# Chunked attention and a multiplicative FFN: scores and values on 64x64 array tiles behind on-chip partition moves, FFN tiles of 512 tokens, first two pairs by halves of heads

## The chip, the cores and the metric

The kernel runs on one core of a Trainium2 chip. Its time is the device time of one execution in microseconds (us); the time before is the median of three executions. Profiles come from one further execution each, recorded by the hardware profiler, which has its own time.

A core has TensorE (PE) for matmuls, with the weight load as a second track (PEld), VectorE (DVE), ScalarE (ACT), GpSimd (POOL), which here only issues loads, and SyncE (SP), which issues the other transfers. Each engine takes its instructions in the order of the program. Matmuls write PSUM; ACT and DVE read it.

## The reference

Two parts follow each other. Attention is local: each of 8 batches x 8 heads has 576 positions of 64 features, cut into 9 chunks of 64 positions, and a position sees only its own chunk.

```python
q_c = q.reshape(B, H, nc, 64, D)          # k_c, v_c alike; B = H = 8, nc = 9, D = 64
scores = (1 / sqrt(D)) * q_c @ k_c.T      # 64 x 64 per chunk and head
attn = exp(scores - max); attn /= sum(attn) + 1e-9
x = (attn @ v_c) put as [4608 tokens, 512 features]
h = ((x @ w1) * (x @ w2)) @ w3            # w1, w2: 512 x 1024; w3: 1024 x 1024
out = h @ w_out                           # w_out: 1024 x 512, float32
```

Inputs and output are float32; inside, operands are bfloat16 and sums float32. Since nothing stands between w3 and w_out, the kernel multiplies these two first and applies their product.

## The kernel before

The 4608 tokens are 72 chunks of 64; two chunks make a unit, and two units make a *pair* of 256 tokens, so there are 18 pairs, 0 to 17. The work is cut into steps with one-letter names, and the string `ORDER` lists them all. A loop at the end of the kernel emits each step's instructions in that order, and a helper (`inorder`) holds the scheduler to it. So the order in `ORDER` is the order in every engine's queue. A step is written as letter, pair, and a second index, as in `T5.1`.

Loads, issued by POOL with a cast to bfloat16: `q`, `k`, `v` load one tensor of a pair, `l` all three; `i` loads a quarter of w1 and of w2, `o` loads w_out, `h` a half of w3. For pair 0 alone q and k come as raw float32 by SP and are cast by ACT (L131, L133).

Attention of a pair:

- `T` (L163): DVE transposes q (`T.0`) or k (`T.1`) in blocks of 32 x 32. The 64 features of a head thereby end as two blocks `e` of 32 over one set of 32 partitions; partition block i (of four) holds chunk i of the pair.
- `S` (L172): scores on PE, by head two steps e of contraction 32, for each of the four chunks: 64 matmuls of 32 rows x 64 columns of weights, 64 wide.
- `E` (L182): exp on ACT. `P` (L188): PE multiplies with v, which has a column of ones for the sums; the queries are cut in two blocks of 32, so 64 matmuls of 64 rows x 32 columns, 65 wide.
- `N` (L204): DVE takes the reciprocal of the sums and scales. `X` (L211): DVE transposes into `xt`, the FFN's right operand, which holds all tokens.

The FFN of a pair, in four steps j of two 128-row blocks of the hidden layer each:

- `A` and `B` (L227): x @ w1 and x @ w2, 8 matmuls each, 256 tokens wide. `C` (L242): ACT copies A's result out of PSUM. `M` (L246): DVE multiplies it with B's into `ab`.
- `O` (L263): PE multiplies `ab` with w3 @ w_out, 16 matmuls 512 wide. `Y` (L279): ACT copies it out and SP stores it. The last pair's O has three pieces with a copy and a store each, all in one PSUM tile.

`V`, `W`, `Z` make w3 @ w_out: DVE transposes w3, PE multiplies, ACT casts. `D` are matmuls on zeros, whose results are overwritten.

Everything on PE writes to one pool of four PSUM tiles (two banks each), taken in turn. Further rings: six qk buffers, seven v buffers, two `qkT`, two `o_sb`, seven `ab`.

In the steady part a pair p reads in `ORDER`: `P(p) M S(p+1) N(p).0 O(p-3) E(p+1) X(p).0 ... A B C M ...`; O of a pair stands right behind the pair's last M and the next S.

Of the kernel before, what the change touches and what calls it, by code (L numbers as in the profile page):

```python
# [9 lines left out]
l0 q1 i0 k1 v1 i1 i2 l2 i3 l3 l4 o h0 h1 l5 D0.0.16.64 T0.0 T0.1 l6 S0 T1.0 E0 P0 D0.1.4.512 T1.1 l7  # L10
N0.0 S1 D1.0.5.512 X0.0 N0.1 X0.1 A0.0 E1 B0.0 C0.0 P1 M0.0 A0.1 N1.0 X1.0 B0.1 C0.1 N1.1 A0.2 X1.1
B0.2 C0.2 M0.1 A1.0 T2.0 B1.0 C1.0 M0.2 A1.1 T2.1 l8 B1.1 C1.1 M1.0 S2 M1.1 A0.3 E2 T3.0 B0.3 C0.3
P2 M0.3 A1.2 N2.0 X2.0 B1.2 C1.2 N2.1 A1.3 X2.1 B1.3 C1.3 M1.2 A2.0 T3.1 l9 B2.0 C2.0 M1.3 S3 T4.0
A2.1 E3 M2.0 B2.1 T4.1 C2.1 P3 l10 M2.1 A2.2 N3.0 B2.2 C2.2 X3.0 A2.3 N3.1 B2.3 X3.1 C2.3 M2.2 S4
M2.3 A3.0 E4 B3.0 C3.0 A3.1 M3.0 B3.1 C3.1 V0 A3.2 M3.1 B3.2 C3.2 V1 A3.3 M3.2 B3.3 C3.3 V2 W0 M3.3
V3 T5.0 W1 Z0 V4 V5 T5.1 W2 Z1 V6 V7 T6.0 P4 l11 Z2 S5 T6.1 W3 E5 N4.0 X4.0 N4.1 X4.1 T7.0 A4.0 Z3
B4.0 T7.1 C4.0 P5 l12 M4.0 S6 N5.0 O0 E6 X5.0 N5.1 X5.1 T8.0 O1 Y0 T8.1 P6 l13 Y1 S7 N6.0 O2 E7 X6.0
N6.1 X6.1 T9.0 T9.1 O3 Y2 A4.1 Y3 B4.1 C4.1 A4.2 M4.1 B4.2 C4.2 A4.3 M4.2 B4.3 C4.3 P7 l14 M4.3 S8
N7.0 O4 E8 X7.0 N7.1 X7.1 T10.0 A5.0 T10.1 Y4 B5.0 C5.0 A5.1 M5.0 B5.1 C5.1 A5.2 M5.1 B5.2 C5.2 A5.3
M5.2 B5.3 C5.3 A6.0 M5.3 B6.0 C6.0 P8 l15 M6.0 S9 N8.0 O5 E9 X8.0 N8.1 X8.1 T11.0 A6.1 T11.1 Y5 B6.1  # L20
C6.1 A6.2 M6.1 B6.2 C6.2 A6.3 M6.2 B6.3 C6.3 P9 l16 M6.3 S10 N9.0 O6 E10 X9.0 N9.1 X9.1 T12.0 A7.0
T12.1 Y6 B7.0 C7.0 A7.1 M7.0 B7.1 C7.1 A7.2 M7.1 B7.2 C7.2 A7.3 M7.2 B7.3 C7.3 P10 l17 M7.3 S11
N10.0 O7 E11 X10.0 N10.1 X10.1 T13.0 A8.0 T13.1 Y7 B8.0 C8.0 A8.1 M8.0 B8.1 C8.1 A8.2 M8.1 B8.2 C8.2
A8.3 M8.2 B8.3 C8.3 P11 M8.3 S12 N11.0 O8 E12 X11.0 N11.1 X11.1 T14.0 A9.0 T14.1 Y8 B9.0 C9.0 A9.1
M9.0 B9.1 C9.1 A9.2 M9.1 B9.2 C9.2 A9.3 M9.2 B9.3 C9.3 P12 M9.3 S13 N12.0 O9 E13 X12.0 N12.1 X12.1
T15.0 A10.0 T15.1 Y9 B10.0 C10.0 A10.1 M10.0 B10.1 C10.1 A10.2 M10.1 B10.2 C10.2 A10.3 M10.2 B10.3
C10.3 P13 M10.3 S14 N13.0 O10 E14 X13.0 N13.1 X13.1 T16.0 A11.0 T16.1 Y10 B11.0 C11.0 A11.1 M11.0
B11.1 C11.1 A11.2 M11.1 B11.2 C11.2 A11.3 M11.2 B11.3 C11.3 P14 M11.3 S15 N14.0 O11 E15 X14.0 N14.1
X14.1 T17.0 A12.0 T17.1 Y11 B12.0 C12.0 A12.1 M12.0 B12.1 C12.1 A12.2 M12.1 B12.2 C12.2 A12.3 M12.2
B12.3 C12.3 P15 M12.3 S16 N15.0 O12 E16 X15.0 N15.1 X15.1 A13.0 Y12 B13.0 C13.0 A13.1 M13.0 B13.1  # L30
C13.1 A13.2 M13.1 B13.2 C13.2 A13.3 M13.2 B13.3 C13.3 P16 M13.3 S17 N16.0 O13 E17 X16.0 N16.1 X16.1
A14.0 Y13 B14.0 C14.0 A14.1 M14.0 B14.1 C14.1 A14.2 M14.1 B14.2 C14.2 A14.3 M14.2 B14.3 C14.3 P17
M14.3 A15.0 N17.0 X17.0 B15.0 C15.0 N17.1 O14 X17.1 M15.0 A15.1 Y14 B15.1 C15.1 A15.2 M15.1 B15.2
C15.2 A15.3 M15.2 B15.3 C15.3 A16.0 M15.3 B16.0 C16.0 O15 M16.0 A16.1 Y15 B16.1 C16.1 A16.2 M16.1
B16.2 C16.2 A16.3 M16.2 B16.3 C16.3 A17.0 M16.3 B17.0 C17.0 O16 M17.0 A17.1 Y16 B17.1 C17.1 A17.2
M17.1 B17.2 C17.2 A17.3 M17.2 B17.3 C17.3 M17.3 O17 Y17
# [4 lines left out]
def kernel(  # L41
# [11 lines left out]
    nc = tc.nc  # L53
# [12 lines left out]
    PT = 2 * UT  # L66
    NP = NT // PT
# [35 lines left out]
    xt = wpool.tile([P, KO, NT], bf, name="xt")  # L103
# [3 lines left out]
    vbuf = [consts.tile([P, 2, H, VW], bf, name=f"vbuf{i}") for i in range(7)]  # L107
# [16 lines left out]
    def load_qk(p, which=(0, 1)):  # L124
        if p not in qk_t:
            qk_t[p] = io.tile([P, 2, H, 2 * D], bf, tag="qk", bufs=6, name="qk")
        for s in which:
            if p == 0:

                raw = io.tile([P, H, 2 * D], f32, tag="raw", name="raw")  # L130
                inorder(nc.sync.dma_start(  # L131
                    raw[:], (q, k)[s][0, :, 0:4 * CH, :].rearrange("h (p t) d -> p h (t d)", t=2)))
                inorder(nc.scalar.copy(qk_t[p][:, s], raw[:]))  # L133
                continue
            for at, b, c, m in spans(4 * p, 4):
                load(qk_t[p][at * BL:(at + m) * BL, s],
                     (q, k)[s][b, :, c * CH:(c + m) * CH, :].rearrange("h (p t) d -> p h (t d)", t=2))

    def load_v(p):
        for u in range(2):  # L140
            for at, b, c, m in spans(4 * p + 2 * u, 2):
                load(vbuf[p % 7][at * CH:(at + m) * CH, u, :, 0:D],
                     v[b, :, c * CH:(c + m) * CH, :].rearrange("h p d -> p h d"))
# [17 lines left out]
    qkT_t, s_t, e_t, pv_t, xn_t = {}, {}, {}, {}, {}  # L161

    def do_T(p, s):  # L163


        if s == 0:
            qkT_t[p] = asb.tile([P, 2, 2, H, CH], bf, tag="qkT", bufs=2, name="qkT")
        inorder(nc.vector.transpose(  # L168
            qkT_t[p][:, s].rearrange("p e h (y t) -> p h t e y", t=2),
            qk_t[p][:, s].rearrange("p h (t e y) -> p h t e y", t=2, e=2)))  # L170

    def do_S(p):  # L172
        qkT = qkT_t.pop(p)
        s_t[p] = s_t.pop(p) if p in s_t else psum("s_ps")
        for h in range(H):
            for e in range(2):
                for i in range(NB):
                    mm(s_t[p][half[i % 2], i // 2, h * CH:(h + 1) * CH],
                       lhsT=qkT[blk[i], 1, e, h, :],
                       rhs=qkT[blk[i], 0, e, h, :], start=(e == 0), stop=(e == 1))  # L180

    def do_E(p):  # L182
        e_t[p] = asb.tile([P, 2, H, CH], bf, tag="e", bufs=2, name="e")
        inorder(nc.scalar.activation(  # L184
            e_t[p][:].rearrange("p u h q -> p u (h q)"), s_t.pop(p)[:],
            Exp, scale=scale, bias=0.0))

    def do_P(p, u):  # L188
        e = e_t[p] if u == 0 else e_t.pop(p)
        pv = pv_t[p, u] = psum("pv")  # L190
        for n in range(2):
            for qh in range(2):
                for g in range(NB):
                    for r in range(2):
                        at = (2 * qh + n) * W
                        mm(pv[blk[g], r, at:at + W],
                           lhsT=e[half[r], u, 2 * g + n, qh * BL:(qh + 1) * BL],
                           rhs=vbuf[p % 7][half[r], u, 2 * g + n, 0:W], start=True, stop=True)

    def do_P2(p):  # L200
        do_P(p, 0)
        do_P(p, 1)

    def do_N(p, u):  # L204
# [3 lines left out]
        xn_t[p, u] = asb.tile([P, 2, 4, D], bf, tag="xn", bufs=2, name="xn")  # L208
        inorder(nc.vector.tensor_mul(xn_t[p, u][:], pv[:, :, :, 0:D], rc.to_broadcast([P, 2, 4, D])))  # L209

    def do_X(p, u):  # L211
        t0 = p * PT + u * UT
        inorder(nc.vector.transpose(  # L213
            xt[:, :, t0:t0 + UT].rearrange("p o (m y) -> p m o y", y=BL),
            xn_t.pop((p, u))[:].rearrange("p r (c n) (z o) -> p (r c) o n z", c=2, o=KO)))

    ab_t, ps_t, a_t = {}, {}, {}
# [9 lines left out]
    def mm_ab(p, j, which):  # L227
        w = (w1, w2)[which]
        for i in range(2):
            for ki in range(KO):  # L230
                mm(ps_t[p, j][:, which, i * PT:(i + 1) * PT],
                   lhsT=w[:, ki, (2 * j + i) * P:(2 * j + i + 1) * P],
                   rhs=xt[:, ki, p * PT:(p + 1) * PT], start=(ki == 0), stop=(ki == KO - 1))

    def do_A(p, j):
        ps_t[p, j] = ps_t.pop((p, j)) if (p, j) in ps_t else psum("ab_ps")
        mm_ab(p, j, 0)

    def do_B(p, j):
        mm_ab(p, j, 1)  # L240
# [5 lines left out]
    def do_M(p, j):  # L246
        if p not in ab_t:
            ab_t[p] = msb.tile([P, FO, PT], bf, tag="ab", bufs=7, name="ab")
        inorder(nc.vector.tensor_mul(  # L249
            ab_t[p][:, 2 * j:2 * j + 2, :].rearrange("p j t -> p (j t)"), a_t.pop((p, j))[:],  # L250
            ps_t.pop((p, j))[:, 1, :]))

    def store(p, u0, u1, n0, n1, o_sb):
        inorder(nc.sync.dma_start(
            out[p * PT + u0 * UT:p * PT + u1 * UT, n0:n1].rearrange("(u p) n -> p u n", p=UT),
            o_sb[:, u0:u1, n0:n1]))

    def mm_o(p, u, n0, n1):
        for ki in range(FO):
            mm(ps_t[p][:, u, n0:n1], lhsT=ab_t[p][:, ki, u * UT:(u + 1) * UT],  # L260
               rhs=w3o[:, ki, n0:n1], start=(ki == 0), stop=(ki == FO - 1))

    def do_O(p):  # L263
        ps_t[p] = psum("o_ps")
        if p < NP - 1:
            for u in range(2):
                mm_o(p, u, 0, DM)
# [89 lines left out]
```

The softmax here doesn't subtract the row's maximum and nothing guards it: scores larger than these inputs give would overflow.

## Time and profile before

| what | value |
|---|---|
| time before, median of 3 | 254.39 us (254.19 to 254.47) |
| the profiled execution, its own time | 254.46 us |
| its span, first to last instruction | 252.7 us |
| granted PE clock | 0.998 of full speed |
| PE busy | 234.9 us, 3841 matmuls |
| DVE, ACT, POOL busy | 156.4, 86.3, 82.9 us |
| DMA of POOL's queue | 18.88 MB written, 82592 packets |
| DMA of SP's queue | 10.49 MB |
| HBM read and written | 38.80 MB, 9.44 MB |

The busiest groups of instructions, as count, busy time and mean duration of one:

| instructions | count | busy us | mean ns |
|---|---|---|---|
| matmuls of A and B, 256 wide | 1136 | 128.0 | 273 |
| matmuls of O, 512 wide | 280 | 63.2 | 379 |
| matmuls of S | 1024 | 11.3 | 193 |
| matmuls of P | 1152 | 12.7 | 197 |
| DVE transposes T | 36 | 45.1 | 1287 |
| DVE products M | 71 | 48.3 | 682 |
| DVE transposes X | 36 | 25.6 | 712 |
| DVE products of N | 36 | 24.9 | 692 |
| ACT copies C | 71 | 41.6 | 586 |
| stores of a pair, 512 KB, issue to landing | 17 | | 4000 |

How to read this. The span lies inside the execution's own time; the rest is before its first and after its last instruction. A matmul's mean duration is longer than its share of PE's time, because matmuls overlap: what counts is the distance between the starts of two. Busy shares are averages over stages. The chain of waits starts at the last instruction and goes back, at each step, to what released it; a piece of the chain carries its start and duration. A window of the timeline merges equal instructions into one line, with start, duration and count. "Idle" of an engine that nobody waits for costs nothing.

### The profile page before, as it was taken

To read this page: it belongs to the slowest core of one execution; us is meant where nothing else is said; L and a number is where in the kernel's file an instruction comes from. 1 tells how busy PE (TensorE), PEld (TensorE's weight loads), DVE (VectorE), ACT (ScalarE), POOL (GpSimd) and SP (SyncE) were. 2 spreads that over 40 slices of the span, in tenths; PEclk is the share of its full clock that TensorE was granted. 3 is DMA by queue.
4 is the path that set the end of the run, shared out by engine and by line. 5 is a ranking of instruction groups with operands and counts; after the bars stand their busy time and mean duration, and the time that the engine had idled before them with its cause. 6 is when DMAs were issued, how large, how long until landed. Compare 5 with 4: busy or idle time off the path is not lost.

```text
span 252.7 us, 8382 instructions
## 1 busy us (share of the span) xinstructions
PE 234.9 (93%) x3841; PEld 170.5 (67%) x3841; DVE 156.4 (62%) x233; ACT 86.3 (34%) x116; POOL 82.9 (33%) x110
## 2 busy tenths in 40 slices
PE   1389999999899999999999999999999999999993
PEld 1237878854555577866868686868686868678662
DVE  1665999699996457486665758584945445432230
ACT  3312424432433343333334243343334332323321
POOL 8756975657984567654020000000000000000000
PEclk9999999999999999999999999999999999999999
DMA  7999999999999999999953020202021120102022
GB/s 177 182 184 177 182 175 202 196 184 167 175 170 214 244 227 182 199 167 148 187 38 92 3 83 4 86 3 86 5 81 44 46 81 5 64 22 84 0 86 83
DMA packets 89763, 29.90 MB, mean 118 GB/s; under 512 B 73728, under 2 KB 85248, under 8 KB 89728
## 3 DMA queue, kind: packets, MB, share of 16 engines
q0 software_dynamic: 82592, 18.88, 80.4%
q1 hardware_dynamic: 7136, 10.49, 11.8%
q8 instruction: 30, 0.49, 0.7%
q14 instruction: 5, 0.04, 0.0%
HBM read 38.80 MB, written 9.44 MB: 191 GB/s over the span
## 4 chain that ended last, share of the span: by engine, by line
PE 65%; DMA 14%; DVE 10%; POOL 4%; ACT 3%; issue 3%; DVEq 0%; POOLq 0%
PE ab_ps L88 39%; PE o_ps L88 25%; DMA w<-in_moe_w_dram 4%; DVE ab L249 4%; DMA qk<-in_q_dram 4%; DMA qk<-in_k_dram 3%; DVE w3T L290 3%; DMA vbuf<-in_v_dram 3%; ACT a_sb L244 3%; POOL w L91 1%; DVE qkT L168 1%; POOL vbuf L91 1%; POOL qk L91 1%; POOL wo L91 1%; DVE xt L213 1%
## 5 line engine op out<-in xcount | busy, mean ns | idle before, releaser
L88 PE MATMUL ab_ps<-xt,w 128*128 128x256 bf16 x1136 | 128.0, 273 | 1.3 <-DVE xt L213 1.3
L88 PEld LDWEIGHTS <-w 128*128 128x128 bf16 x1152 | 112.3, 98 | 19.4 <-DVE xt L213 2.4
L249 DVE TENSOR_TENSOR ab<-a_sb,ab_ps 128x512 bf16<-128x512 f32 x71 | 48.3, 682 | 71.6 <-ACT a_sb L244 71.6
L244 ACT COPY a_sb<-ab_ps 128x512 f32<-128x512 f32 x71 | 41.6, 586 | 79.3 <-PE ab_ps L88 79.3
L88 PE MATMUL o_ps<-w3o,ab 128*128 128x512 bf16 (+1 forms) x296 | 65.3, 373 | 2.7 <-ACT o_sb L276 1.1
L88 PEld LDWEIGHTS <-ab 128*128 128x128 bf16 x296 | 28.7, 97 | 33.3 <-issue 1.6
L168 DVE STREAM_TRANSPOSE qkT<-qk 128x1024 bf16<-128x1024 bf16 x36 | 45.1, 1287 | 8.5 <-ACT qk L133 5.1
L91 POOL DMA_DIRECT2D vbuf<-in_v_dram x40 | 33.9, 852 | 31.3 <-PE pv L88 16.3
L283 ACT COPY o_sb<-o_ps 128x1024 f32<-128x1024 f32 x17 | 17.2, 1014 | 45.9 <-PE o_ps L88 43.2
L213 DVE STREAM_TRANSPOSE xt<-xn 128x512 bf16<-128x512 bf16 x36 | 25.6, 712 | 1.2
L209 DVE TENSOR_TENSOR xn<-pv,rc 128x512 bf16<-128x512 f32 x36 | 24.9, 692 | 1.2
L91 POOL DMA_DIRECT2D qk<-in_q_dram x23 | 18.1, 793 | 6.8 <-DMA qk<-in_k_dram 2.4
L184 ACT ACTIVATE e<-s_ps 128x1024 bf16<-128x1024 f32 x16 | 16.4, 1025 | 8.7 <-PE s_ps L88 8.4
L91 POOL DMA_DIRECT2D qk<-in_k_dram x23 | 18.0, 788 | 3.3 <-DMA w<-in_moe_w_dram 1.7
L88 PEld LDWEIGHTS <-qkT 32*64 32x64 bf16 x1152 | 11.4, 111 | 10.6 <-DVE qkT L168 9.6
L88 PE MATMUL w_ps<-wo,w3T 128*128 128x512 bf16 x64 | 14.2, 379 | 0.0
L88 PEld LDWEIGHTS <-e 64*32 64x32 bf16 x1152 | 10.1, 90 | 5.5 <-issue 3.6
L88 PE MATMUL pv<-vbuf,e 64*32 64x65 bf16 x1152 | 12.7, 197 | 1.1 <-ACT e L184 1.1
L91 POOL DMA_DIRECT2D w<-in_moe_w_dram x16 | 11.1, 697 | 5.4 <-DMA wo<-in_moe_w_out_dram 3.0
L88 PE MATMUL s_ps<-qkT 32*64 32x64 bf16 x1024 | 11.3, 193 | 0.0
L88 PEld LDWEIGHTS <-w3T 128*128 128x128 bf16 x64 | 6.2, 98 | 7.1
L290 DVE STREAM_TRANSPOSE w3T<-w 128x1024 bf16<-128x1024 bf16 x8 | 9.6, 1211 | 0.9 <-DMA w<-in_moe_w_dram 0.9
(20 smaller groups left out, 33.9 us busy)
## 6 DMA issues: line engine op xcount, KB each, us to landing
out_dram<-o_sb SPq DMA_DIRECT2D x17, 512.0 KB, 4.0
vbuf<-in_v_dram POOLq DMA_DIRECT2D x32, 128.0 KB, 6.7
w<-in_moe_w_dram POOLq DMA_DIRECT2D x16, 256.0 KB, 9.9
qk<-in_q_dram POOLq DMA_DIRECT2D x11, 256.0 KB, 6.6
qk<-in_k_dram POOLq DMA_DIRECT2D x11, 256.0 KB, 8.0
wo<-in_moe_w_out_dram POOLq DMA_DIRECT2D x4, 256.0 KB, 6.9
qk<-in_q_dram POOLq DMA_DIRECT2D x4, 192.0 KB, 9.4
qk<-in_k_dram POOLq DMA_DIRECT2D x4, 192.0 KB, 8.7
```

Source lines behind the costliest of these rows:

```text
L88: return inorder(nc.tensor.matmul(*a, **kw))
L91: return inorder(nc.gpsimd.dma_start(dst, src))
L168: inorder(nc.vector.transpose(qkT_t[p][:, s].rearrange("p e h (y t) -> p h t e y", t=2), qk_t[p][:, s].rearrange("p h (t e y) -> p h t e y ...
L184: inorder(nc.scalar.activation(e_t[p][:].rearrange("p u h q -> p u (h q)"), s_t.pop(p)[:], Exp, scale=scale, bias=0.0))
L209: inorder(nc.vector.tensor_mul(xn_t[p, u][:], pv[:, :, :, 0:D], rc.to_broadcast([P, 2, 4, D])))
L213: inorder(nc.vector.transpose(xt[:, :, t0:t0 + UT].rearrange("p o (m y) -> p m o y", y=BL), xn_t.pop((p, u))[:].rearrange("p r (c n) (z o) ...
L244: inorder(nc.scalar.copy(a_t[p, j][:], ps_t[p, j][:, 0, :]))
L249: inorder(nc.vector.tensor_mul(ab_t[p][:, 2 * j:2 * j + 2, :].rearrange("p j t -> p (j t)"), a_t.pop((p, j))[:], ps_t.pop((p, j))[:, 1, :]))
L283: inorder(nc.scalar.copy(o_sb[:], ps_t.pop(p)[:]))
L290: inorder(nc.vector.transpose(w3T_t[f][:].rearrange("p k (f y) -> p f k y", y=BL), w3[:, NB * f:NB * (f + 1), :].rearrange("p f (k x) -> p ...
```

## The change

Four things change together, with a new `ORDER`.

1. *First two pairs by halves of heads.* `q`, `k`, `T`, `S`, `E`, `P` of pairs 0 and 1 come twice, with four heads each. q and k of pair 0 are loaded by POOL like all others; the raw transfers on SP and the casts on ACT are gone. Of the zero matmuls `D`, 32 of 64 columns stay ahead of S0; those of 512 columns ahead of A0.0 are gone.
2. *From pair 8 on, q, k and x of two pairs change partitions.* A group g is two pairs, 2g and 2g+1; `qkT` now holds both pairs of a group. `G` (new) moves it by SP transfers from `qkT` to `qkm`, so that the two blocks e of a head's features stand one above the other on 64 partitions. A score then needs one matmul of 64 x 64 instead of two of 32 x 64. `P` takes all 64 queries of a chunk as weights: 64 x 64. Its output then has another layout, so `X` writes to `xm`, and `H` (new) moves that to `xt` by SP transfers. Each `G` and each `H` has two halves of four transfers: 32 partitions of 4 KB each (128 KB) for G, of 2 KB each (64 KB) for H.
3. *Loads run five pairs ahead*, with five qk and six v buffers instead of six and seven.
4. *FFN tiles of 512 tokens from pair 4 on.* A and B work for a whole group, 8 steps j with one 128-row block each: 4 matmuls of 512 columns. `ab` and `xt` become rings by group (three and four buffers). From pair 8 on M writes `ab` in runs of 32 tokens to undo the order that H left. O stands later, apart from its M. The store of `Y` becomes a step of its own, `Q`. The last O's three pieces take a PSUM tile each, and Y16 with its Q16 stands behind that O.

The diff, cut to its core:

```diff
 ORDER = """
-l0 q1 i0 k1 v1 i1 i2 l2 i3 l3 l4 o h0 h1 l5 D0.0.16.64 T0.0 T0.1 l6 S0 T1.0 E0 P0 D0.1.4.512 T1.1 l7
...
-C10.3 P13 M10.3 S14 N13.0 O10 E14 X13.0 N13.1 X13.1 T16.0 A11.0 T16.1 Y10 B11.0 C11.0 A11.1 M11.0
...
-M17.1 B17.2 C17.2 A17.3 M17.2 B17.3 C17.3 M17.3 O17 Y17
+q0.0 k0.0 q0.1 k0.1 v0 q1.0 q1.1 k1.0 k1.1 i0 v1 q2 k2 i1 v2 i2 i3 q3 k3 v3 o h0 h1 q4 k4 v4
+D0.0.32.64 T0.0.0 T0.1.0 T0.0.1 S0.0 T0.1.1 q5 k5 v5 E0.0 S0.1 E0.1 P0.0 P0.1 T1.0.0 N0.0 T1.1.0
+T1.0.1 S1.0 T1.1.1 q6 k6 v6 E1.0 X0.0 S1.1 N0.1 X0.1 P1.0 E1.1 T2.0 A0.0 T2.1 q7 k7 B0.0 C0.0 P1.1
+v7 M0.0 A0.1 N1.0 B0.1 C0.1 X1.0 S2 N1.1 E2 M0.1 X1.1 P2 A1.0 N2.0 B1.0 X2.0 C1.0 A1.1 N2.1 B1.1
...
+M3.2 B3.3 C3.3 V3 W0 M3.3 T4.0 W1 Z0 V4 V5 T4.1 q9 k9 v9 W2 Z1 V6 V7 T5.0 S4 Z2 W3 T5.1 q10 k10 E4
+T6.0 T6.1 P4 v10 q11 k11 Z3 S5 N4.0 O0 E5 X4.0 N4.1 X4.1 T7.0 O1 T7.1 Y0 Q0 T8.0 P5 v11 q12 k12 Y1
+S6 T8.1 O2 Q1 E6 N5.0 X5.0 N5.1 X5.1 O3 T9.0 T9.1 Y2 G4.0 P6 v12 q13 k13 A4.0 N6.0 B4.0 G4.1 Y3 X6.0
+N6.1 C4.0 A4.1 X6.1 B4.1 C4.1 M4.0 Q2 S7 Q3 M4.1 A4.2 E7 T10.0 B4.2 C4.2 T10.1 P7 v13 q14 k14 A4.3
+M4.2 B4.3 N7.0 C4.3 A4.4 X7.0 M4.3 B4.4 C4.4 N7.1 A4.5 M4.4 B4.5 C4.5 X7.1 S8 M4.5 S9 E8 A4.6 T11.0
...
+M16.6 B16.7 C16.7 O13 M16.7 O14 Y13 Q13 O15 Y14 Q14
+O16 Y15 Q15 O17 Y16 Q16 Y17 Q17
 """
...
+    def move(dst, src):
+        inorder(nc.sync.dma_start(dst, src))
...
+    def do_G(g, a):
+        if a == 0:
+            qkm_t[g] = asb.tile([P, 2, 2, 2, H, CH], bf, tag="qkm", bufs=2, name="qkm")
+        for i in (2 * a, 2 * a + 1):
+            for e in range(2):
+                move(qkm_t[g][blk[2 * a + e], i % 2], qkT_t[g][blk[i], e])
...
+            else:                                                     # do_S, pair 8 on
+                for i in (0, 3, 1, 2):
                     mm(s_t[p][half[i % 2], i // 2, h * CH:(h + 1) * CH],
+                       lhsT=qkm_t[g][half[i // 2], i % 2, m, 1, h, :],
+                       rhs=qkm_t[g][half[i // 2], i % 2, m, 0, h, :], start=True, stop=True)
...
+                else:                                                 # do_P, pair 8 on
+                    for g, r in ((0, 0), (1, 1), (1, 0), (0, 1)):
+                        mm(pv[half[g], r, m * W:(m + 1) * W], lhsT=e[half[r], u, 4 * g + m, :],
+                           rhs=vbuf[p % 6][half[r], u, 4 * g + m, 0:W], start=True, stop=True)
...
+    def do_H(g, a):
+        xt = new_xt(g)[:].rearrange("p (s c) -> p s c", s=2)
+        for k_ in range(2):
+            for i in (2 * a, 2 * a + 1):
+                move(xt[blk[2 * a + k_], i % 2], xm_t[g][blk[i], k_].rearrange("p o m t -> p (o m t)"))
...
+    def do_AB(p, j, f, which):
...
+        fs = (f,) if p >= 4 else (2 * j, 2 * j + 1)
+        n = GT // len(fs)
+        for i, f in enumerate(fs):
             for ki in range(KO):
+                mm(ps_t[p, j][:, which, i * n:(i + 1) * n],
+                   lhsT=(w1, w2)[which][:, ki, f * P:(f + 1) * P], rhs=rhs[:, ki],
+                   start=(ki == 0), stop=(ki == KO - 1))
...
+        else:                                                         # do_M, pair 8 on
+            o = ab_t[g][:, j].rearrange("p (c s y) -> p s c y", s=2, y=BL)
+            view = lambda t: t.rearrange("p (s c y) -> p s c y", s=2, y=BL)
+        inorder(nc.vector.tensor_mul(o, view(a_t.pop((p, j))[:]), view(ps_t.pop((p, j))[:, 1, :])))
...
+            t = psum("o_ps")                                          # do_O, last pair: a tile for each piece
+            mm_o(t[:, 0, 0:n1 - n0], p, u, n0, n1)
+            inorder(copy(o_sb[:, u, n0:n1], t[:, 0, 0:n1 - n0]))
+            store(p, u, u + 1, n0, n1, o_sb[:, u:u + 1, n0:n1])
```

## The prediction, made before the changed kernel ran

> **What bounds the kernel now.** I read the engine shares first, then the busy times by stage, then the chain of waits, then the rows of single steps on TensorE (PE), last the DMA rows. The two page lines show PE busy for 93% of the span, and the DMA engines nearly full for the first half of it.
>
> ```profile
> PE 234.9 (93%) x3841; PEld 170.5 (67%) x3841; DVE 156.4 (62%) x233; ACT 86.3 (34%) x116; POOL 82.9 (33%) x110
> DMA  7999999999999999999953020202021120102022
> ```
>
> The stages (busy time of each engine in a stretch) say where PE is not full: 10.5 us before 18.26, under 1 us in each stretch up to 212, and 4.5 us at the end. From 18.26 to 212 the path is PE's own instructions, one after the other.
>
> ```profile
> 0.00:18.26 18.26, 7.78 (x217) 4.51 (x218) 8.96 (x18) 5.43 (x5) 12.75 (x21) 1.00 1.44 181
> 18.26:52.25 33.99, 33.33 (x641) 28.15 (x640) 27.21 (x40) 11.87 (x18) 23.83 (x33) 1.00 1.66 187
> 52.25:68.29 16.04, 15.38 (x194) 7.26 (x191) 15.90 (x20) 5.28 (x6) 12.18 (x16) 1.00 1.99 173
> 68.29:128.10 59.81, 59.28 (x1008) 41.54 (x1008) 39.71 (x57) 21.40 (x28) 32.41 (x41) 1.00 1.66 187
> 128.10:212.00 83.90, 82.98 (x1457) 62.77 (x1456) 52.30 (x80) 30.69 (x42) 1.76 (x2) 1.00 0.18 49
> 212.00:252.70 40.70, 36.17 (x330) 26.21 (x328) 12.27 (x20) 11.62 (x18) 0.00 (x0) 0.99 0.14 53
> ```
>
> The chain gives the price of each PE step: P and S 0.63 and 0.64 us (64 small matmuls each), A and B together 7.00 us for 64 of 256 columns (109 ns each), O 3.45 us for 16 of 512 columns (216 ns each). It also shows, once in every pair, a detour over ACT and DVE ahead of O: O waits for the last product M.
>
> ```profile
> 78.68 0.63 PE pv L88 x64
> 79.30 0.64 PE s_ps L88 x64
> ...
> 121.19 7.00 PE ab_ps L88 x64
> 128.20 0.02 issue
> 128.22 0.59 ACT a_sb L244
> 128.81 0.02 issue
> 128.84 0.70 DVE ab L249
> 129.53 0.04 issue
> 129.58 3.61 PE o_ps L88 x16
> ...
> 225.07 3.45 PE o_ps L88 x16
> ```
>
> **Small matmuls (pairs 8 to 17).** S falls from 64 matmuls of 32 rows by 64 to 32 of 64 by 64; P from 64 of 64 by 32 to 32 of 64 by 64. Whether half the count takes half the time depends on what paces a block. Two timeline answers, cut off at 128.90 and 128.19, count the matmuls started from the block's start to the cut:
>
> ```profile
> 128.74 0.35 PE L88 MATMUL s_ps<-qkT 32*64 32x64 bf16 x20
> 128.11 0.26 PE L88 MATMUL pv<-vbuf,e 64*32 64x65 bf16 x17
> ```
>
> S starts 20 in 160 ns on four tiles: one round of four each 32 ns. P starts 17 in 80 ns on eight tiles: a round of eight each 35 to 40 ns. So a round costs some 32 to 40 ns however many tiles it has, and the count alone does not pace it. The new blocks have 8 rounds of four tiles: 8 x 32 = 0.26 us, and the 0.13 us that S has beyond its 16 rounds (0.64 - 16 x 0.032): 0.385 us for S, 0.39 for P. Saved: 10 x (1.27 - 0.775) = 5.0 us, all on the path. Bounds: half of the old time, 6.3 us; nothing, 0. A rule speaks against it: by the Trainium skill, "TensorE: Matmul & The Clock Gate", section "The mechanism", a weight load overlaps running matmuls only in other row groups, and by "LDWEIGHTS (loading the stationary operand)" 64 columns take 64/1.2 = 53 ns. Two of the four new tiles share each half of the rows, so a round would be an estimated 2 x (53 + 64/2.4 = 27 of streaming) = 160 ns and a block 1.28 us: 20 blocks x 0.64 = 12.8 us lost, and the sum below would end at 266. The P row says no: four tiles share a row half there, 128 weight columns per half and round as in the new form, in 35 to 40 ns. I take the row.
>
> **512-column tiles.** 14 pairs from pair 4 on trade 64 matmuls of 109.1 ns for 32 of 215.7: 6.98 - 6.90 = 0.08 us each, 1.1 us. ACT copies and DVE products stay 512 wide, at 586 and 682 ns against a PE step of 1.73 us for A and B. From pair 8 M writes runs of 32 elements; the nearest row is the strided xn product of the same size, 692 ns, so I cost it at nothing, hidden by PE; at 900 ns DVE would come late a few times, some 1.7 us in all.
>
> **O apart from its M.** From pair 4 on O comes well after its ab. S to O starts take 0.84 us where S to A take 0.64: 0.2 us by nine later pairs, 1.8 us gone. In the last O the wait for M (0.25) and the two waits for copies of the same PSUM tile (the waits list has PE o_ps after ACT o_sb at 1.1 us) go: 1.3 us. Entering a block of small matmuls costs about 0.1 us (the chain's B before P takes 0.97 instead of 0.87 at the matmul starts); from A4.0 on there are 17 entries instead of 13: +0.4.
>
> **Start to O3.** SP's two raw transfers (landed at 5.09 and 6.95) and two ACT casts go; all loads come from POOL. In before POOL's first packet moved at 5.60, though issued at 1.24 to 2.25, as SP's megabyte drained; a store issued at 76.30 behind loads also landed only at 83.70. I take it that a newcomer waits for what is queued, so loads now flow from about 2.5. Consecutive landings give the service times: 1.43 us for q or k of a pair, 0.72 for half, 1.30 for a quarter of w, 0.85 for half of v. k of pair 1 lands at about 10.7 (13.77 before), its transpose, X0.0, N0.1 and X0.1 take 3.0 us, A0.0 starts near 14 to 15 (18.26). But A0.1 now waits for its weights near 19, and A1.0 for X1.1, which stands on DVE behind T2.1 (k of pair 2 at 17.9, +1.3) and 4.6 us of M, N and X: 23.8 against 25.34, with 0.5 us less work done by then. Lead 1.0. Before's waits of 0.85 (A4.0 on xt) and 0.2 (O0) go too, a new one of 0.3 (A2.0 on xt) comes: 1.7; I take 1.5 for the removed warm-up matmuls (before, A0.0 ran at half speed). w3 is no limit: without pair 4 ahead of it its half lands near 43, before 48.86.
>
> **What is added.** Ten groups of eight transfers on SP, G and H for five pairs of pairs. G waits for the four T of its group, H for its four X; behind them on SP stand the stores Q2 to Q5, and on DVE T12.0, T14.0 and T16.0 now wait for the landing of G4 to G6 (the qkT buffer), with products M behind them. Between S8, which needs G4 too, and T12.0 stand some 13 us of PE work, so I cost that at nothing. G4 is issued after T9.1; S8 stands behind P6, six steps A and B, S7 and P7, 0.63 + 10.4 + 1.27 = 12.3 us. SP issues one in 0.37 us with at most eight in flight, 3 us for eight; the first may sit 7.4 us in the queue as that store did: 10.5, just in time. G5 and G6 run under the last loads with about the same lead, G7 and G8 after them. Nearest rows:
>
> ```profile
> out_dram<-o_sb SPq DMA_DIRECT2D x2, 128.0 KB, 1.7
> DMA to landing us min/median/max: 1.7/2.8/7.4
> ACT o_sb L283 <- DMA out_dram<-o_sb: 2.7, 1, 2.7
> ```
>
> A piece of 128 KB then costs some 0.37 us of the engines (512 less 128 KB is 1.1 us, 2.8 - 1.7). By the skill's "DMA: Bandwidth & Descriptors", section "Anatomy of one DMA — SWDGE (gpsimd) path", one transfer costs 2.0 us + bytes/436 GB/s: an estimate of 2.3 us, eight in a row 18 us, 6 us over the lead in each of five groups, +30. The 1.7 us of the store and SP's 0.37 us spacing speak for overlap. Bounds 0 and 7; taken 1.2. Stores Q queue behind G and H on SP: with two o_sb buffers Y3 waits for store 1, and A4.1 for Y3's PSUM: +0.9 (before shows one such wait, 2.7). POOL issues the same bytes; five qk and six v buffers instead of six and seven let a load start one pair later at most (v of pair 10 now waits for P4), which DMA backlog hides until pair 11 and PE's lead after that: nothing.
>
> **End.** Y16 now stands on ACT behind the copies of O17, and its 512 KB store on SP behind O17's three: issued 0.4 us after the last small one, it lands 2.8 us and two 128 KB shares later: 4.3 us after the last matmul instead of 2.2: +2.1.
>
> **Sum**, against the profiled execution (254.46 us, span 252.7; the median of the three is 254.39): -1.5 -5.0 -1.1 -1.8 -1.3 +0.4 +1.2 +0.9 +2.1 = -6.1: 248.4.
>
> **Rivals.**
> 1. The moves decide, and it is slower. If a 32-partition piece takes 0.85 us of the engines instead of 0.37, eight take 6.8 us and with the queue 14 us, over the 12.3 of lead; SP's later groups then run into each other. S8, S10 and S12 would wait 3, 2.5 and 5 us, 10.5 in all against the 1.2 counted: 257.7. It decides against before from 7.3 us of such waits. For it: 32 partitions on each side, DMA full until 128. Against: wo's loads write 256 KB to 32 partitions at the usual 1.3 us.
> 2. The packing gives nothing (blocks paced by weight columns, which P keeps): 248.4 + 5.0 = 253.4. For it: S and P took the same before with different tiles. Against: the counts above.
> 3. POOL's first packet is late for reasons of its own and loads flow from 5.6 again: +3.1, 251.5.
> 4. No queueing, moves and stores hidden (-2.1), the lead at A1.0 kept whole (-0.5): 245.8.
>
> **How the numbers follow.** Forecast 0.50 (247 to 250), rival 1 0.12, rival 2 0.09, rival 3 0.15, rival 4 0.14. Slower by over 0.2% (what a measurement of this kernel can tell from no change) is rival 1 save its mild end: 0.11; 0.03 within, where rivals 2 and 3 add up; 0.86 faster. The range 245.0 to 254.0 takes in rivals 2 to 4 and the bounds of packing; rival 1 lies outside.
>
> **What would show it.** In the profile after: first POOL packet near 2.5; A1.0 near 24; S and P blocks of 32 at 0.38 to 0.40 us; O without a DVE wait ahead of it; S8, S10, S12 with no wait on DMA qkm; a last store of 512 KB ending the chain. Waits of PE on qkm or xt DMAs of more than 2 us a group make rival 1 true, blocks still at 0.6 us rival 2, A1.0 after 26 rival 3.

## The result and the profile after

The changed kernel takes 251.17 us (median of four runs, 250.8 to 252.59) against 254.29 (254.05 to 254.47): a ratio of 0.9888, 95% interval 0.9848 to 0.9928. The forecast was 248.4, so the change brought 3.1 us of the 6 expected. Its profiled execution took 251.03 us with a span of 249.3; that of before, 254.46 and 252.7. Both leave 1.8 us outside the span, so the two spans can be compared step by step.

The page rows of engine time and DMA, after:

```profile
PE 226.9 (91%) x2740; PEld 122.0 (49%) x2760; DVE 154.5 (62%) x236; ACT 83.4 (33%) x116; POOL 86.9 (35%) x116
DMA  7999999999999999999999974635502200400334
```

The program issues 1081 matmuls fewer (2760 instead of 3841; 20 records are missing from this trace) and PE is busy 8 us less, yet its share of the span fell. So the span holds more idle PE time than before. The busy times by stage tell where:

```profile
0.00:19.48 19.48, 6.23 (x257) 5.20 (x257) 9.12 (x21) 3.67 (x5) 16.20 (x26) 1.00 1.40 128
19.48:54.57 35.09, 33.29 (x552) 27.80 (x546) 27.04 (x41) 10.82 (x17) 22.14 (x31) 1.00 1.61 190
128.00:212.00 84.00, 82.93 (x738) 38.55 (x741) 47.31 (x75) 30.53 (x44) 1.25 (x2) 1.00 0.55 118
212.00:249.30 37.30, 32.20 (x156) 15.26 (x156) 5.93 (x9) 10.61 (x15) 0.00 (x0) 0.98 0.26 97
```

The columns are length, then busy time (and count) of PE, PEld, DVE, ACT and POOL, granted clock, DMA share, GB/s. The first row ends at A0.0, as the first row of before did at 18.26: A0.0 comes 1.2 us later. It moves 128 GB/s where before moved 181, though POOL issues loads through 16.2 of its 19.5 us. The second row ends at W0, which before reached at 52.25. The middle is as full as before, and the last row has 5.1 us without PE instead of 4.5.

With three marks, the starts of W0 and of the last matmul and the end of the span, the difference splits exactly (S4's 0.64 us stood before W0 and now stands behind it):

| stretch | before | after | measured | forecast |
|---|---|---|---|---|
| start to W0, without S4 | 51.61 | 54.57 | +2.96 | -0.5 |
| W0 to the last matmul, with S4 | 197.53 | 189.47 | -8.06 | -7.75 |
| last matmul's start to the end | 3.55 | 5.22 | +1.67 | +2.1 |
| sum | 252.69 | 249.26 | -3.43 | -6.1 |

The forecast column takes the terms of the prediction's sum to where they belong. Ahead of W0: the lead of 1.0 less 0.3 for A2.0 and 0.2 for the warm-up. Behind W0: all others and the 1.05 us of waits at A4.0 and O0.

The loads come no sooner than before. The transpose of k of pair 1 starts when the data have landed, before and then after (where they come by halves, the first at 13.61 and the second at 14.30):

```profile
13.79 1.30 DVE L168 STREAM_TRANSPOSE qkT<-qk 128x1024 bf16<-128x1024 bf16 x1 [2.77 <-DMA qk<-in_k_dram]
...
13.63 1.94 DVE L177 STREAM_TRANSPOSE qkT<-qk 128x512 bf16<-128x512 bf16 x3 [0.88 <-DMA qk<-in_k_dram]
```

The prediction had k of pair 1 at 10.7 instead of 13.77. The chain of waits begins so, in start, duration, what:

```profile
1.24 3.12 POOL qk L96 x4
...
9.72 7.24 DMA w<-in_moe_w_dram
...
17.24 7.36 DMA w<-in_moe_w_dram
24.65 1.05 PE ab_ps L93 x8
...
26.47 1.03 ACT e L209
...
27.54 0.70 PE pv L93 x64
```

A0.1 starts at 23.28, its weights landed at 23.23; B0.1 starts at 24.65, when its own land, one transfer later. Behind B0.1 stand S2, E2, P2, and only then A1.0, at 28.18. The prediction had the weights of A0.1 near 19 and A1.0 at 23.8; its service times put the weights of B0.1 near 20.5.

The small matmuls are as forecast, or better. Two timeline rows of PE, S8 with S9 and then P8:

```profile
99.09 0.71 PE L93 MATMUL s_ps<-qkm 64*64 64x64 bf16 x64
...
101.56 0.45 PE L93 MATMUL pv<-vbuf,e 64*64 64x65 bf16 x32
```

The next block starts 0.64 us after the first and 0.38 after the second: 0.32 for a pair's S, 0.38 for its P.

The moves: the row of G's transfers with its landing times, and S14, one of the two places where PE waits for them (its block is stretched from 0.5 to 1.4 us; the other is S12, whose block starts at 133.60 and is stretched from 0.5 to 1.3):

```profile
L169 SPq DMA_DIRECT2D qkm<-qkT x40: 507/592/1662, 83.7 to 158.4; - x40
DMA to landing us min/median/max: 2.3/7.2/8.4
...
148.96 0.93 PE L93 MATMUL s_ps<-qkm 64*64 64x64 bf16 x63 [0.41 <-DMA qkm<-qkT]
```

### The profile page after: what moved, and what is told of

It reads as the page before. It is cut to its first block, busy times and chain, and to the rows that moved or that the text cites. A ratio compares the mean times of both kernels' runs of the same rounds, so it can differ in the third digit from the quotient of the medians.

```text
span 249.3 us, 6372 instructions
## 1 busy us (share of the span) xinstructions
PE 226.9 (91%) x2740; PEld 122.0 (49%) x2760; DVE 154.5 (62%) x236; ACT 83.4 (33%) x116; POOL 86.9 (35%) x116
## 4 chain that ended last, share of the span: by engine, by line
PE 73%; DMA 17%; POOL 3%; DVE 2%; issue 1%; ACT 1%; SPq 0%; DVEq 0%; ACTq 0%; POOLq 0%
PE ab_ps L93 41%; PE o_ps L93 22%; DMA out_dram<-o_sb 6%; DMA w<-in_moe_w_dram 6%; PE w_ps L93 6%; DMA qkm<-qkT 5%; PE s_ps L93 3%; PE pv L93 2%; POOL qk L96 2%; DVE qkT L177 1%; POOL vbuf L96 1%; ACT e L209 0%; DVE ab L321 0%; POOL w L96 0%; ACT a_sb L306 0%
## 5 line engine op out<-in xcount | busy, mean ns | idle before, releaser
L93 PE MATMUL ab_ps<-xt,w 128*128 128x512 bf16 (+1 forms) x697 | 130.0, 343 | 1.1 <-DMA w<-in_moe_w_dram 0.5
L93 PEld LDWEIGHTS <-w 128*128 128x128 bf16 x704 | 67.8, 99 | 55.6 <-DMA w<-in_moe_w_dram 0.9
L177 DVE STREAM_TRANSPOSE qkT<-qk 128x1024 bf16<-128x1024 bf16 (+1 forms) x40 | 45.6, 1178 | 11.0 <-DMA qk<-in_q_dram 8.3
L209 ACT ACTIVATE e<-s_ps 128x1024 bf16<-128x1024 f32 (+1 forms) x18 | 17.1, 978 | 8.9 <-PE s_ps L93 8.7
L93 PE MATMUL pv<-vbuf,e 64*32 64x65 bf16 (+1 forms) x832 | 11.0, 200 | 4.5 <-DMA vbuf<-in_v_dram 3.3
L93 PEld LDWEIGHTS <-e 64*32 64x32 bf16 (+1 forms) x832 | 8.3, 99 | 11.5 <-issue 6.6
L236 DVE RECIPROCAL rc<-pv 128x8 f32<-128x8 f32 x36 | 6.9, 192 | 11.3 <-PE pv L93 11.2
L259 DVE STREAM_TRANSPOSE xm<-xn 128x512 bf16<-128x512 bf16 x20 | 13.6, 697 | 0.2
L251 DVE STREAM_TRANSPOSE xt<-xn 128x512 bf16<-128x512 bf16 x16 | 11.3, 707 | 0.4
L93 PEld LDWEIGHTS <-qkT 32*64 32x64 bf16 x512 | 5.8, 116 | 11.2 <-DVE qkT L177 9.2
```

The lines of the kernel that those rows point to most:

```text
L93: return inorder(nc.tensor.matmul(*a, **kw))
L177: inorder(nc.vector.transpose(qkT_t[g][:, :, p % 2, s, heads(h)].rearrange("p e h (y t) -> p h t e y", t=2), qk_t[p][:, s, heads(h)].rearr ...
L209: inorder(nc.scalar.activation(e_t[p][:, :, heads(hh)], s_t[p][:].rearrange("p u (h q) -> p u h q", q=CH)[:, :, heads(hh)], Exp, scale=sca ...
L236: inorder(nc.vector.reciprocal(rc[:], pv[:, :, :, D:W]))
L251: inorder(nc.vector.transpose(new_xt(g)[:].rearrange("p (o t) -> p o t", o=KO)[:, :, t0:t0 + UT] .rearrange("p o (m y) -> p m o y", y=BL), ...
L259: inorder(nc.vector.transpose(xm_t[g][:, u, :, m].rearrange("p o (c y) -> p c o y", y=BL), xn_t[p][:].rearrange("p u r m d -> p (u r) m d" ...
```

## The experiments

Times are medians; the ratio to before has its 95% interval. "k of pair 1" is the landing of its last transfer; in the changed kernel it is at 14.30 us. In the kernels that take the raw path, the branch for pair 0 in `load_qk` is that of before (raw tile, SP transfer, ACT copy).

**1. The start of before.** With the raw branch, and the old part of `ORDER` up to W0:

```diff
-q0.0 k0.0 q0.1 k0.1 v0 q1.0 q1.1 k1.0 k1.1 i0 v1 q2 k2 i1 v2 i2 i3 q3 k3 v3 o h0 h1 q4 k4 v4
-D0.0.32.64 T0.0.0 T0.1.0 T0.0.1 S0.0 T0.1.1 ...
+q0 k0 v0 q1 i0 k1 v1 i1 i2 q2 k2 v2 i3 q3 k3 v3 q4 k4 v4 o h0 h1
+D0.0.16.64 T0.0 T0.1 q5 k5 v5 S0 T1.0 E0 P0 D0.1.4.512 T1.1 q6 k6 v6 N0.0 S1 D1.0.5.512 ...
```

> The changed kernel with the start of the kernel before: q and k of pair 0 raw through SP with ACT casts, whole heads, the old order of loads and steps up to W0, both groups of 512-wide matmuls on zeros; from W1 on everything as changed, and pair 4's scores stay after W0. If the start is what the sum got wrong (in the changed kernel W0 begins at 54.57 us, before at 52.25), W0 comes at 51 to 52 and the time falls by 2.5 to 3.5, to about 248. If instead later steps give the gain back (moves, stores, the end), W0 moves and the time does not: 250.5 to 251.5.

Measured: 248.68 us, ratio 0.9779 (0.9757 to 0.9801). W0 at 52.12. Its stage from A0.0 to W0:

```profile
18.14:52.12 33.98, 32.66 (x577) 27.50 (x576) 24.05 (x37) 10.84 (x17) 23.53 (x32) 1.00 1.66 187
```

From A4.0 to the last matmul's start it takes 157.78 us, the changed kernel 157.61: nothing else moved. The start lost 2.5 us, and the rest of the change needs none of it. W0 still comes 0.5 us later than before (51.61); why is not shown.

**2. Whole loads for pairs 0 and 1,** the steps still by halves:

```diff
-q0.0 k0.0 q0.1 k0.1 v0 q1.0 q1.1 k1.0 k1.1 i0
+q0 k0 v0 q1 k1 i0
```

> The changed kernel with q and k of pairs 0 and 1 loaded whole (4 POOL transfers for them instead of 8), the transposes, scores and values still by halves. Theory of the issue: a half costs POOL 0.77 us and a whole one 0.89, so loads then flow faster, k of pair 1 lands 1.5 to 2 us sooner than 14.30, A0.0 starts at 18 or before, and the time falls by about 1.5. Theory of the order (pair 2's q and k and the second quarter of w stand before A1.0) and theory of the raw path (one queue alone can't feed the engines): A1.0 stays within 0.7 us of 28.18, and the time within 0.5 of the changed kernel's 251.

Measured: 250.01 us, ratio 0.9810 (0.9778 to 0.9842). k of pair 1 lands at 11.77, A0.0 starts at 17.39, A1.0 at 26.35, W0 at 53.15, 1.4 us sooner. From 4 to 12 us POOL's queue moves 0.67 and 0.73 MB in 4 us, against 0.54 and 0.57. The loads by halves cost this much, by landing and by time.

**3. The raw path for pair 0 alone:**

```diff
-q0.0 k0.0 q0.1 k0.1 v0
+q0 k0 v0                      # pair 0 raw through SP, cast by ACT
```

> The changed kernel with q and k of pair 0 as before: raw float32 through SP and cast by ACT; all else is as changed, pair 1 by halves. Theory of the raw path: two queues move more in the first 16 us, all later landings come 1.5 to 2.5 us sooner, A1.0 starts near 26 and the time falls by about 2. Theory of the issue: six transfers fewer by four only (q and k of pair 0), so half of the gain of whole heads, under 1 us. Theory of the order: A1.0 near 28, 251.

Measured: 248.79 us, ratio 0.9763 (0.9741 to 0.9785). k of pair 1 lands at 11.21, although its halves stand there as in the changed kernel; A1.0 at 26.14, W0 at 52.62. Its chain:

```profile
6.79 7.09 DMA w<-in_moe_w_dram
...
14.17 8.40 DMA w<-in_moe_w_dram
...
22.62 1.05 PE ab_ps L93 x8
...
25.51 0.70 PE pv L93 x64
```

The same pieces as after, 2 us earlier. This one edit gives back almost all that the old start gives. Yet even so the weights of B0.1 land at 22.57 and not near 20.5, where the service times of the prediction put them.

**4. The zero matmuls of 512 columns put back:**

```diff
-P0.0 P0.1 T1.0.0 ... S1.1 N0.1
+P0.0 P0.1 D0.1.4.512 T1.0.0 ... S1.1 D1.0.3.512 N0.1
```

> The changed kernel with matmuls on zeros of 512 columns put back: four after the values of pair 0, three ahead of pair 1's. In the changed kernel the first 16 matmuls of A0.0 and B0.0 go at 201 ns each, before at 150 (with five such matmuls ahead), later at 110. If the missing matmuls cost, A0.0 gains 0.8 us and A1.0 comes as much sooner, 250.3. If the loads set A1.0 (the second quarter of w lands after 24.6), nothing moves: 251.

Measured: 252.03 us, ratio 0.9902 (0.9873 to 0.9931), not to be told apart from the changed kernel by its time, which could hide a gain of some tenths of a microsecond. Four timeline rows of this kernel: zero matmuls, then 16 of A0.0 and B0.0, then A0.1, then B1.1:

```profile
15.51 1.46 PE L93 MATMUL z_ps<-zero 128*128 128x512 bf16 x3
...
19.08 3.59 PE L93 MATMUL z_ps<-xt,w 128*128 128x256 bf16 x16
...
23.92 1.05 PE L93 MATMUL ab_ps<-xt,w 128*128 128x256 bf16 x8 [0.81 <-DMA w<-in_moe_w_dram]
...
33.27 2.90 PE L93 MATMUL ab_ps<-xt,w 128*128 128x256 bf16 x25 [1.76 <-issue]
```

The 16 still go at 211 ns each, later ones at 110, and A0.1 waits for weights either way. So the zero matmuls here warmed nothing, and what they could save is hidden under the load: the prediction's 0.2 for them was no error that matters. W0 comes at 56.70 in this trace, 2.1 later than in the changed kernel. Most of that is the pause of 1.76 us ahead of B1.1; `issue` means that PE waited for nothing that the profile shows (more on this in the last section).

**5. Whole loads for pair 0 only:**

```diff
-q0.0 k0.0 q0.1 k0.1 v0 q1.0 q1.1 k1.0 k1.1
+q0 k0 v0 q1.0 q1.1 k1.0 k1.1
```

> The changed kernel with q and k of pair 0 loaded whole through POOL, those of pair 1 still by halves. Theory that halves are slow only while the queue is empty (as the first transfers): from 4 to 12 us POOL's queue moves 0.67 to 0.73 MB in 4 us as with whole tensors, against 0.54 to 0.57 in the changed kernel, and k of pair 1 lands complete at 12 to 12.5 us (11.8 with both pairs whole, 14.3 in the changed kernel). Theory that halves are slow wherever they stand: it lands at 13 or later.

Measured (one profiled execution): 250.29 us. k of pair 1 lands at 12.14, and its four halves come 0.72 us apart (9.97, 10.69, 11.44, 12.14), just the service time that the prediction assumed. From 4 to 12 us: 0.66 and 0.72 MB in 4 us. W0 at 53.04. Halves are not slow in themselves; they are slow as the first transfers.

**6. Y16 and its store ahead of O17:**

```diff
-O16 Y15 Q15 O17 Y16 Q16 Y17 Q17
+O16 Y15 Q15 Y16 Q16 O17 Y17 Q17
```

> The changed kernel with Y16 and its store ahead of O17. By the working of the prediction the end then has only the last small store behind it: from the last matmul's start to the end of the span 3.5 us as before instead of 5.23, and the time is 1.7 lower, 249.4. If Y16's copy on ACT delays the copies of O17, or if the megabyte of stores is what ends late anyway, less than 0.7.

Measured: 249.58 us, ratio 0.9797 (0.9778 to 0.9816). From the last matmul's start to the end 3.68 us instead of 5.22. The changed kernel's chain ends so, and 4.4 us of its span lie behind the copy, where only stores are under way:

```profile
238.08 6.24 PE o_ps L93 x36
...
244.40 0.42 DVE o_sb L344
```

**7. No packing and no moves:** the forms of pairs 0 to 7 for all pairs, G and H left out of `ORDER`.

```diff
-            if p < 8:          # do_S, do_P, do_X, do_M; in do_AB p >= 8 alike
+            if p < 18:
```

> The changed kernel without the packing: pairs 8 to 17 take the scores, values and x as pairs 0 to 7 do (64 small matmuls each, x straight into xt), and G and H are gone. The trace of the changed kernel shows S at 0.32 and P at 0.37 us there, so 10 x (1.27 - 0.69) = 5.8 us come back, less the 0.6 us wait at S14: 256.2. Rival (the moves hold up more than the trace shows, by contention with the loads and by what waits behind them on SP): well under that, 253 or less; if packing gives nothing, 251.

Measured: 257.2 us, ratio 1.0096 (1.0076 to 1.0115): 6.0 us more than the changed kernel by the medians. From A4.0 to the last matmul's start 163.77 us against 157.61, 6.2 more. S8 with S9 and P8 in this kernel:

```profile
98.97 1.27 PE L92 MATMUL s_ps<-qkT 32*64 32x64 bf16 x128
...
103.24 0.68 PE L92 MATMUL pv<-vbuf,e 64*32 64x65 bf16 x62 [1.04 <-issue]
```

Against 0.71 and 0.45 us in the rows of after. A pair's S and P take 0.60 and 0.63 us here, 0.32 and 0.38 there: 5.3 us for ten pairs. Two more differences go opposite ways: the waits for moves, 1.8 us, are gone, and pauses that the profile gives to `issue`, like the 1.04 above, stretch blocks by 2.8 us more (3.5 in all, 0.7 in after). So the 6 us are what packing and moves together are worth in this program, not the price of the blocks alone. Without them it is slower than before.

**8. Another order of steps,** with the raw path, the end of experiment 6 and three zero matmuls:

```diff
-P2 A1.0 N2.0 B1.0 X2.0 C1.0 A1.1 ...
+A1.0 B1.0 C1.0 P2 N2.0 A1.1 M1.0 B1.1 X2.0 C1.1 N2.1 A0.2 ...
```

> A better start and end on the changed kernel: q and k of pair 0 raw through SP with ACT casts, three 512-wide matmuls on zeros between S1.1 and P1.0, P2 behind A1.0 and B1.0, A0.2 ahead of A2.0, Y16 and its store ahead of O17. From the raw path alone 248.8; if PE then waits neither for E2 ahead of P2 (1.4 us) nor for X2.1 ahead of A2.0 (0.6), and the end gives its 1.7: 245.3. If the loads of w and of pair 2 set the pace of the first 30 us instead of the order of steps, only the end gains: 247.

Measured: 249.60 us, ratio 0.9798 (0.9778 to 0.9817): a miss. A1.0 starts at 27.17, after 2.0 us in which PE waits for X1.1 on DVE; P2, now behind it, comes at 29.02 instead of 25.5. Later waits of 0.4 us (for xt) and 0.9 (for qkT) follow, and W0 is at 55.43, later than in the changed kernel. Moving P2 behind A1.0 had looked like removing a wait for E2; that wait covered another. But the zero matmuls delay X1.1 too: A0.0 starts at 18.56 with them, 17.42 in experiment 3, and X1.1 ends at 27.11 instead of 25.98. An estimate from these: without them the exchange would bring A1.0 to about 26.0, against 26.14 there, next to nothing.

**9. Three edits together:** raw path, the end of experiment 6, Q4 and Q5 behind G7.

```diff
-O5 N11.0 N11.1 Q4 X11.0 ... T15.1 Q5 A8.3 ... G7.1 P12
+O5 N11.0 N11.1 X11.0 ... T15.1 A8.3 ... G7.1 Q4 Q5 P12
```

> The changed kernel with three edits that the runs so far point to: q and k of pair 0 raw through SP with ACT casts, stores Q4 and Q5 behind G7, Y16 and its store ahead of O17. If the parts add up: raw path 248.8, end -1.6, the wait of S14 for G7 (0.6 us in the changed kernel) gone: 246.6 to 247.2. If G7 is late for its own transposes and not for the stores in SP's queue, the wait at S14 stays at 0.6.

Measured: 246.92 us, ratio 0.9703 (0.9678 to 0.9728). The parts add up: W0 at 52.19, the end 3.55 us. The waits at S12 and S14 are all but gone, but one of 1.1 us between two matmuls stands at S10, ahead of the stores that were moved; from A4.0 to the last matmul's start it takes 157.47 us, 0.14 less than in the changed kernel. The S10 wait varies between traces (0.3 us in that of experiment 6), so what the order of the stores is worth alone is not shown.

**10. The old start with k of pair 1 ahead of w,** and the same end and store order:

```diff
-q0 k0 v0 q1 i0 k1 v1 i1 i2 ...     P0 D0.1.4.512 T1.1
+q0 k0 v0 q1 k1 i0 v1 i1 i2 ...     P0 T1.1 D0.1.1.512
```

> The same end and store order, on the start of the kernel before (raw path, whole heads, old order of steps), with k of pair 1 loaded ahead of the first quarter of w and the zero matmuls behind T1.1. With the start of before alone W0 came at 52.1 with k of pair 1 landed at 13.65; here k lands near 11.2, the first A goes at 16 instead of 18.1, A0.1 with its weights at 19 instead of 21.1, so W0 at 50 to 51 and the time 245.0 to 246. If the weights pace this start whatever the order, W0 stays at 52 and the time is 246.6 to 247.

Measured: 246.32 us, ratio 0.9675 (0.9655 to 0.9696), the fastest of all: 3.2% under before. A0.0 starts at 15.88, but W0 only at 51.63, half a microsecond sooner than with the start of before. Two pieces of its chain, and the second as the timeline has it:

```profile
30.59 1.31 DVE qkT L182
...
35.67 1.92 PE ab_ps L92 x16
...
35.67 1.92 PE L92 MATMUL ab_ps<-xt,w 128*128 128x256 bf16 x16 [1.25 <-DVE xt L256]
```

q of pair 3 lands at 30.57; its transpose stands on DVE ahead of the scaling and the transposes of pair 2, for which PE waits 1.25 us. What was won at A0.0 is mostly lost there.

**11. Each transfer of G twice,** the second into a tile that nothing reads:

```diff
                 move(qkm_t[g][blk[2 * a + e], i % 2], qkT_t[g][blk[i], e])
+                move(qkx_t[g][blk[2 * a + e], i % 2], qkT_t[g][blk[i], e])
```

> The changed kernel with each transfer of G issued twice, the second time into a tile that nothing reads: 16 transfers of 128 KB in a group instead of 8. It measures the margin of the moves. SP issues one in 0.64 us, so a group's last landing comes 5 us later, and what stands behind it on SP too. By the trace of the changed kernel PE waits for a move once, 0.6 us at S14; if that is because the lead is near used up (the prediction's rival of late moves was close), S8, S10, S12 and S14 each wait 2 to 5 us and the time rises by over 8. If there is margin of several us, it rises by under 4.

Measured (one profiled execution): 270.94 us, 19.9 more. The waits list now has

```profile
PE s_ps L93 <- DMA qkm<-qkT: 15.9, 4, 5.7
```

at S8, S10, S12 and S14. The granted clock was 0.969 over the span (0.997 in the changed kernel), so the 19.9 are not waits alone: its clock records stand at half three times, for 3.4, 6.8 and 3.4 us from 102.4, 143.4 and 167.3, each behind such a wait. The margin of the moves is small.

**12. Halves by chunks instead of by heads,** in the same order:

```diff
-                load(qk_t[p][at * BL:(at + m) * BL, s, heads(h)], ...      # 128 partitions x 4 heads
+                load(qk_t[p][at * BL:(at + m) * BL, s], ...                # 64 partitions x 8 heads
```

> The changed kernel with q and k of pairs 0 and 1 loaded in halves of the same size (128 KB written) and in the same order, but split by chunks (64 partitions, eight heads) instead of by heads (128 partitions, four heads). It tells whether the slow start (k of pair 1 complete at 14.3 us, 0.54 to 0.57 MB moved in 4 us) comes from the number of transfers into an empty queue or from the shape of a half of heads. Number: k of pair 1 again lands at 14 to 14.5. Shape: at 12 to 12.5, as with pair 0 whole. The first scores wait for both halves here, so S0 comes later by up to 1.5 us; the time says little.

Measured (one profiled execution): 250.04 us; k of pair 1 lands at 13.05, between the two expectations; 0.56 and 0.62 MB in 4 us. Inconclusive: the first transfers are slow in both shapes, less so here. POOL issued such a half in about 0.70 us and a half of heads in about 0.77. In the changed kernel the first ten transfers (nine landings are in the trace) did not land evenly: six distances are 0.7 to 0.85 us, just the service time, and three are 1.7 to 1.8 (behind 4.60, 8.68 and 11.93). The first landed 3.4 us after its issue and the last 6.0, so issuing at 0.77 us a piece is not the pace alone. What opens the three gaps stays open.

## Why the prediction was wrong, point by point

The step that failed is "Start to O3", taken as -1.5. Ahead of W0 it measured +2.96 where -0.5 was forecast: 3.5 us, more than the whole difference between 248.4 and 251.2. The other terms together came out 0.7 us better than forecast, in part because errors cancel: packing (5.7 instead of 5.0) and stores (nothing instead of 0.9) were better, the moves worse (1.6 instead of 1.2), and S7 is stretched by 0.7 us in a pause that no term had.

- *First packet near 2.5.* Right: POOL's first packet moved at 2.84, before at 5.60. The third rival's mechanism did not happen, though its number (251.5) did, and its mark, A1.0 after 26: a mark that two causes share does not tell them apart.
- *"So loads now flow from about 2.5", at 0.72 us for half a tensor.* Wrong. The service times came from rows where transfers stood queued; at the start of the changed kernel the first ten transfers landed 1.1 us apart on average (4.60 to 14.30). Experiments 2, 3 and 5 show that three different ways of having no half first (whole tensors, pair 0 on SP) bring k of pair 1 to 11.2 to 12.1 instead of 14.30, and W0 1.4 to 1.95 us forward. SP's megabyte, which the prediction saw only as what POOL waits behind, was a part of the faster start: it moved from 1.85 us on, while POOL was still issuing. But of the 2.45 us that W0 gains with the old start (54.57 to 52.12), whole tensors from POOL alone give 1.5 (experiment 5), and SP's transfers of pair 0 0.4 more (experiment 3).
- *Weights of A0.1 near 19.* They landed at 23.23. In the changed kernel nearly all of that was lost by k of pair 1, 3.6 us late; from there on it took 8.9 us where 8.5 was counted. With the raw path the later part was off too: from k of pair 1 to the weights of B0.1, 11.4 us where 9.8 was counted. The working laid service times end to end. But landings have gaps: 13.89 to 16.31 there, where 0.85 was counted, and 3.3 us for the pair of w transfers up to 22.57 (behind k of pair 2 at 19.24), where 2.6 was. The rows of before had such a gap too, from 15.51 to 17.95 where 1.30 was counted, and it was passed over.
- *Lead at A1.0.* From the weights of B0.1, through B0.1, S2, E2 and P2, to A1.0 it takes 3.5 us (24.65 to 28.18 after, 22.62 to 26.14 in experiment 3). From 20.5 that leads to 24.0, near the 23.8 forecast: the landings failed, not this path. Experiment 8 shows no way around it: behind P2 stands the wait for X1.1, and the exchange of steps mostly moves the wait.
- *Warm-up matmuls.* Experiment 4: no effect on the 16 matmuls, and the wait for weights hides it anyway.
- *Packing -5.0, from counted rounds.* Too small: the blocks took 0.32 and 0.38 instead of 0.385 and 0.39. From 1.27 to 0.70 for ten pairs is 5.7 us, and experiment 7 prices packing less moves at about 6, pauses included. The counted row was the right choice over the rule cited from the Trainium skill, "TensorE: Matmul & The Clock Gate", section "The mechanism", which led to 1.28 us for a block and to 266 for the sum. The second rival is out.
- *512-column tiles, O apart, O17.* A and B of a group take 13.81 us for 64 matmuls (215.8 ns each), the O waits for M are not in the chain: as forecast.
- *Moves +1.2.* Measured: S12 stretched by 0.8 us and S14 by 0.8, 1.6 in all. But the agreement is luck. SP spaces moves by 0.64 us, not 0.37, and each takes 7.2 us to land, so G4 needs 12.1 us from first issue to last landing, not 10.5. Its lead was larger too: S8 came 15.4 us after the first issue, 3.4 after the last landing. For S10 that margin is 0.4 us, and S12 and S14 have none. Nor did G7 run after the last loads: they ended at 148.0, 14.4 us later than before, and G7, issued from 136.8 on, took 7.4 us a transfer under them, G8 2.3 to 2.4 behind them. Experiment 11 shows what lies beyond it. The first rival was nearer than its 0.12.
- *Stores +0.9.* The wait of Y3 is there (4.0 us on ACT) but PE shows no wait for PSUM after A4.0: zero.
- *End +2.1.* Measured +1.67, and experiment 6 gives 1.5 of it back with one exchange in `ORDER`.

## What to carry over

Service times taken from a backlog hold in a backlog: at the start of a kernel, look at when the first bytes of each queue move and how fast landings follow each other while the queue is still short, and carry over the gaps that the trace before already shows. A transfer on a second queue that seems to hold up the first can be what fills the engines while the first is still issuing: take it away alone, before building on its absence. And keep a last large store ahead of the last small ones.

## What was not expected of the hardware

- Ten transfers of 128 KB, first in an empty queue, moved 0.54 MB in 4 us, against 0.66 to 0.73 with whole tensors in front; the same halves behind a megabyte of another queue, or behind two whole tensors, landed every 0.72 us. Three gaps of 1.7 to 1.8 us make the difference; what opens them is not settled (experiment 12).
- The instruction queue of the trace carries 22 packets of 16 KB, 0.9 to 1.5 us each. In every start looked at, one of them falls beside a gap in the landings of loads: packet at 15.68 in before (landings 15.51, 17.95), 11.48 after (11.93, 13.61), 14.13 in experiment 3 (13.89, 16.31), 13.25 in experiment 2 (13.11, 15.61); in experiments 1, 5 and 12 alike. That is a coincidence seen seven times, not an experiment.
- PE's unexplained pauses (`issue`) go with the same packets. All that last over 0.15 us, in all changed kernels, end 2.2 to 2.8 us after the start of such a packet and stand at the same few places of the program, whatever the time: S7's 0.52 us at 91.04 behind a packet at 88.49, experiment 4's 1.76 at 33.27 behind 31.02, experiment 7's 1.04 at 103.24 behind 100.74. There is about one packet for every 250 to 260 matmuls and weight loads (22 for 5520 after, 30 for 7682 before), so it looks as if PE waits there for its own instructions. Against it: before has more of these packets and no such pause. No experiment varied this.
- The first 16 matmuls of A0.0 and B0.0 took 200 to 211 ns each and later ones 110, while the clock column says 1.00 for that stage. But the trace's clock records begin only at 22.30 after and at 19.51 before, and there the distance of matmul starts falls from 213 to 109 ns; ahead of them the 1.00 stands for no record. Five zero matmuls of 512 columns right ahead made the average 150 in before (6 slow ones, 13 or 14 after); three of them with half a microsecond of small or no matmuls behind did not help in experiment 8.
- Transfers from SBUF to SBUF of 128 KB over 32 partitions land 7.2 us after issue (the median) while loads run, and 2.3 to 2.4 us once they have ended (G8).
